# Decays made two units ahead, with two cumulative sums per unit and the third sum replaced by products with w on GpSimd

## The chip, the cores and the metric

The kernel runs on one core of a Trainium2 chip. The metric is the time of one execution on the device in microseconds (us). A profile gives a span, from the first to the last instruction. It is about 1.8 us shorter than the time of the same execution. An execution is called slow when it takes over 1.5% more than the fastest of the same kernel. PE is TensorE (matmuls), DVE is VectorE, ACT is ScalarE, POOL is GpSimd. SBUF is the on-chip memory, PSUM the memory that takes the results of matmuls.

## The reference, cut to what matters

A linear attention with a decay per channel is followed by a two-layer GELU network.

```python
# r, k, v, w: (4 batches, 8 heads, 768 tokens, 48); u: (8, 48); w is between 0.8 and 0.95
for t in range(S):
    cur = einsum('bhd,bhe->bhde', u * k[t], v[t])
    y[t] = einsum('bhd,bhde->bhe', r[t], state + cur)
    state = w[t][..., None] * state + einsum('bhd,bhe->bhde', k[t], v[t])
x = y as (3072 tokens, 384)
out = gelu_tanh(x @ w_in) @ w_out        # w_in 384 x 2048, w_out 2048 x 384
```

## The kernel before

The kernel cuts the work into 12 units, each of 256 tokens of one batch. A partition holds two neighbouring tokens, called t = 0 and t = 1. In a chunk of 128 tokens (64 partitions) the recurrence becomes matmuls: k is divided by the product of the decays up to its token, r is multiplied by it, and the scores are products of the two. The products of decays are exponentials of cumulative sums of log w, and a matmul with a triangular matrix makes such a sum.

For two tokens per partition there are three sums: x (before the first token), y (with the first token), z (with both). The excerpts below show this stage. Cuts are marked with `...`.

```python
def a1(q):                       # PE: three cumulative sums, two matmuls each
    x, y, z = (ps_a.tile([P, 512], FP, ...) for i in range(3))
    for dst, s0, s1 in ((x, strict, strict), (y, incl, strict), (z, incl, incl)):
        PE.matmul(dst[:, 0:HD], s0, lw[:, 0, :, 0:D], start=True, stop=False)
        PE.matmul(dst[:, 0:HD], s1, lw[:, 1, :, 0:D], start=False, stop=True)
    ...
def exps(q):                     # ACT: exp(-y), exp(-z), exp(x), exp(y), and a small one
    ...
def prep(q):
    # DVE: two multiplies of 128x768
    DVE.tensor_tensor(out=kk[:, :, :, 0:D], in0=tdh(kt), in1=dec(e1), op=AL.mult)
    DVE.tensor_tensor(out=rq[:, :, :, 0:D], in0=tdh(rt), in1=dec(fq), op=AL.mult)
    # POOL: v to bf16, k*r, times u, and the decay of the state (am)
    POOL.tensor_copy(out=vb, in_=tdh(vt))
    POOL.tensor_tensor(out=rk, in0=kt..., in1=rt..., op=AL.mult)      # one buffer
    POOL.tensor_tensor(out=rk, in0=rk, in1=u_bc..., op=AL.mult)
    for c2 in range(2):
        POOL.tensor_tensor(out=am[:, c2], in0=blk..., in1=al..., op=AL.mult)
def prep_b(q):                   # DVE: sum over the channels; POOL: times v
    DVE.tensor_reduce(out=dg, in_=rk, axis=AX.X, op=AL.add)
    POOL.tensor_tensor(out=vsc, in0=vb, in1=dg..., op=AL.mult)
def a2(q, which):                # PE: transposes of kk or rq; DVE: copy TT out of PSUM
    ...

for q in range(NU):              # unit q: the network (mm1, mm2); unit q+1: attention
    att = attention(q + 1)       # a2, a2, then scores, y, state, xs, xT
    table("gelu")
    for i in range(8):
        mm1(q, i)                # expansion, 6 matmuls, then a GELU on ACT
        if i >= 2: mm2(q, 0, ...)        # second projection, first half
        next(att) ...
        if i == 6: a1(q + 2)
    table("exp")
    exps(q + 2); ln(q + 3)
    mm2(q, 0, range(12, 16))
    store(q, 0)
    prep(q + 2); prep_b(q + 2)
    mm2(q, 1, range(16))         # 16 matmuls
    store(q, 1)
```

For units 0 and 1 the loop has another order (all eight expansions first), and the weights of the network are cast to bf16 in between.

## Time and profile before

The median is 235.81 us over four runs (235.05 to 238.04).

The first three lines are from the page of the kernel before: busy time of each engine with its share of the span, and two rows of the picture in 40 slices of 5.9 us (tenths of busy PE, tenths of the clock that PE was granted). The clock row reads 9 in the first five slices too, but there the sums' matmuls start 0.32 us apart (23.88 and 24.20 us) where a steady unit has 0.16 us, so PE ran at half speed there and the row does not show it.

```profile
PE 203.4 (86%) x2448; PEld 143.0 (61%) x2448; DVE 131.3 (56%) x211; ACT 134.0 (57%) x223; POOL 104.5 (44%) x87
PE   0456787598895999999999999999999999999992
PEclk9999996779997999999999999999999999999998
```

PE is the busiest engine. Its row shows two parts: about 13 slices in which it often stands still, and a steady part at 9. An average over both hides that the limits differ.

I therefore read from the PE timeline where each unit's first expansion group starts. The differences are the time that each unit takes (its "stretch" below; in the steady part, its "period"):

| kernel before | unit 0 | unit 1 | unit 2 | unit 3 | each of units 3 to 6 | end of span |
|---|---|---|---|---|---|---|
| start, us | 24.8 | 53.7 | 74.0 | 91.3 | 16.56 per unit | 235.9 |

The start takes 91.3 us for three units, and the rest takes 144.6 us for nine. The next line is the windows view of the kernel before for one steady unit: window, its length, busy time of PE, PEld (weight loads), DVE, ACT, POOL with the number of instructions, then the granted clock, the DMA share and GB/s.

```profile
107.90:124.50 16.60, 15.93 (x211) 11.45 (x209) 10.22 (x17) 10.55 (x20) 8.22 (x6) 1.00 0.54 121
```

PE works 15.93 of 16.60 us. The two places where it does not are in the PE timeline of the kernel before (start, duration, instruction, and in brackets the idle time before it and what ended it):

```profile
110.63 0.82 PE L345 MATMUL h_2_1683<-xT_1595,w_in_sb 128*128 128x256 bf16 x6 [0.36 <-ACT g_1644 L347]
118.80 0.32 PE L170 MATMUL cum_1_1847<-logw_122,incl 128*128 128x384 bf16 x1 [0.31 <-ACT xs_1844 L321]
```

The third expansion waits for a GELU, and the second cumulative sum waits for a buffer that the copy of y frees.

These are the two decay multiplies of unit 0 in the kernel before (DVE timeline):

```profile
8.27 0.96 DVE L202 TENSOR_TENSOR kk_125<-k_91,e_219 128x768 bf16<-128x768 f32 x1 [1.04 <-ACT e_219 L184]
9.14 1.58 DVE L203 TENSOR_TENSOR rq_127<-r_93,fq_218 128x768 bf16<-128x768 f32 x1
```

The two are alike in shape and type, yet the second takes 1.58 us and the first 0.96.

### The profile page before, as it was taken

How to read it: one execution, taken by the hardware profiler on the slowest of the kernel's cores; microseconds unless marked ns; L12 is line 12 of the kernel's file. 1: busy time of each engine (PE TensorE's matmuls, PEld its weight loads, DVE VectorE, ACT ScalarE, POOL GpSimd, SP SyncE). 2: the span in 40 equal slices, each digit the busy share in tenths (PEclk: the TensorE clock that was granted, in tenths of full speed). 3: DMA queues.
4: the chain of work that ended last, by engine and by line, in shares of the span. 5: the costliest groups of instructions: out<-in, count | busy, mean ns of one | idle time of the engine just before them, and what ended most of it. 6: DMA issues, size and time to landing. Idle time of an engine off the chain costs nothing.

```text
span 235.9 us, 5759 instructions
## 1 busy us (share of the span) xinstructions
PE 203.4 (86%) x2448; PEld 143.0 (61%) x2448; DVE 131.3 (56%) x211; ACT 134.0 (57%) x223; POOL 104.5 (44%) x87
## 2 busy tenths in 40 slices
PE   0456787598895999999999999999999999999992
PEld 0334564357564767667767667676777677677761
DVE  7684686561636538547547747656285376374200
ACT  3433780566255449459368377395494684765670
POOL 3473792639008504806708509329158076060000
PEclk9999996779997999999999999999999999999998
DMA  7999999713902911942923914915719120020202
GB/s 173 307 396 297 331 320 255 160 33 72 231 15 54 246 25 36 206 98 53 232 56 75 257 24 111 210 33 124 182 35 212 24 62 10 13 56 0 68 1 67
DMA packets 56969, 30.45 MB, mean 129 GB/s; under 512 B 50928, under 2 KB 56176, under 8 KB 56944
## 3 DMA queue, kind: packets, MB, share of 16 engines
q1 hardware_dynamic: 56944, 30.09, 52.1%
q8 instruction: 19, 0.31, 0.6%
q14 instruction: 6, 0.05, 0.1%
HBM read 25.36 MB, written 4.72 MB: 127 GB/s over the span
## 4 chain that ended last, share of the span: by engine, by line
PE 54%; ACT 19%; DVE 11%; issue 9%; POOL 3%; DMA 2%; DVEq 0%; ACTq 0%; POOLq 0%
ACT L156 5%; DVE w_out_sb L86 2%; DMA w_89<-in_w_dram 2%; PE o_0_532 L354 1%; DVE rq_127 L203 1%; ACT logw_124 L162 1%; PE o_0_3678 L354 1%; PE o_0_3457 L354 1%; PE o_0_3175 L354 1%; PE o_1_3740 L354 1%; PE o_1_3632 L354 1%; PE o_1_3389 L354 1%; POOL rk_418 L210 1%; POOL rk_418 L212 1%; ACT logw_122 L162 1%
## 5 line engine op out<-in xcount | busy, mean ns | idle before, releaser
L345 PEld LDWEIGHTS <-w_in_sb 128*128 128x128 bf16 x576 | 54.0, 99 | 21.1 <-issue 9.9
L156 ACT ACT_TABLE_LOAD x13 | 16.7, 1283 | 0.9 <-PEq L487 0.7
L158 ACT ACT_TABLE_LOAD x12 | 15.4, 1283 | 0.2
L171 PEld LDWEIGHTS <-strict 128*128 128x128 bf16 x24 | 2.5, 104 | 9.9 <-issue 9.5
L215 POOL TENSOR_TENSOR am_997<-blk,al_975 128x384 f32<-128x384 bf16 x2 | 2.4, 1230 | 12.5 <-ACT al_975 L187 12.5
L215 POOL TENSOR_TENSOR am_1304<-blk,al_1273 128x384 f32<-128x384 bf16 x2 | 2.4, 1229 | 11.5 <-ACT al_1273 L187 11.5
L215 POOL TENSOR_TENSOR am_1608<-blk,al_1577 128x384 f32<-128x384 bf16 x2 | 2.4, 1230 | 8.3 <-ACT al_1577 L187 8.3
L215 POOL TENSOR_TENSOR am_1912<-blk,al_1881 128x384 f32<-128x384 bf16 x2 | 2.4, 1230 | 8.3 <-ACT al_1881 L187 8.3
L215 POOL TENSOR_TENSOR am_2216<-blk,al_2185 128x384 f32<-128x384 bf16 x2 | 2.4, 1230 | 8.3 <-ACT al_2185 L187 8.3
L215 POOL TENSOR_TENSOR am_2520<-blk,al_2489 128x384 f32<-128x384 bf16 x2 | 2.4, 1228 | 8.3 <-ACT al_2489 L187 8.3
L215 POOL TENSOR_TENSOR am_2811<-blk,al_2780 128x384 f32<-128x384 bf16 x2 | 2.4, 1228 | 7.9 <-ACT al_2780 L187 7.9
L215 POOL TENSOR_TENSOR am_3100<-blk,al_3069 128x384 f32<-128x384 bf16 x2 | 2.4, 1228 | 7.9 <-ACT al_3069 L187 7.9
L215 POOL TENSOR_TENSOR am_3382<-blk,al_3352 128x384 f32<-128x384 bf16 x2 | 2.4, 1228 | 7.9 <-ACT al_3352 L187 7.9
L354 PE MATMUL o_0_532<-w_out_sb,g_437 128*128 128x384 bf16 x16 | 5.5, 469 | 0.2 <-ACT w_out_sb L84 0.2
L236 PEld LDWEIGHTS <-rq_127 128*128 128x128 bf16 x48 | 3.4, 104 | 3.3 <-DVE rq_127 L203 3.2
L354 PEld LDWEIGHTS <-g_437 128*128 128x128 bf16 x32 | 3.3, 117 | 3.2 <-issue 2.5
L170 PE MATMUL cum_0_201<-logw_122,strict 128*128 128x384 bf16 x1 | 0.5, 479 | 5.4 <-ACT logw_122 L162 5.4
L362 DVE COPY ob_3736<-o_0_3678 128x384 f32<-128x384 f32 x1 | 0.6, 558 | 7.7 <-PE o_0_3678 L354 7.7
L215 POOL TENSOR_TENSOR am_699<-blk,al_677 128x384 f32<-128x384 bf16 x2 | 2.3, 1187 | 4.3 <-ACT al_677 L187 4.3
L354 PEld LDWEIGHTS <-g_3653 128*128 128x128 bf16 x32 | 3.0, 98 | 1.7 <-ACT g_3653 L347 0.4
L238 DVE COPY TT_1_818<-T_1_809 128x1024 bf16<-128x1024 bf16 x1 | 0.7, 692 | 6.0 <-PE T_1_809 L236 6.0
L354 PE MATMUL o_0_3678<-w_out_sb,g_3653 128*128 128x384 bf16 x16 | 3.8, 327 | 0.0
(942 smaller groups left out, 694.2 us busy)
## 6 DMA issues: line engine op xcount, KB each, us to landing
wi_155<-in_moe_w_in_dram SPq DMA_DIRECT2D x1, 512.0 KB, 5.0
wi_157<-in_moe_w_in_dram SPq DMA_DIRECT2D x1, 512.0 KB, 6.0
wi_159<-in_moe_w_in_dram SPq DMA_DIRECT2D x1, 512.0 KB, 6.7
wi_161<-in_moe_w_in_dram SPq DMA_DIRECT2D x1, 512.0 KB, 7.5
wi_163<-in_moe_w_in_dram SPq DMA_DIRECT2D x1, 512.0 KB, 8.7
wi_165<-in_moe_w_in_dram SPq DMA_DIRECT2D x1, 512.0 KB, 9.6
w_89<-in_w_dram SPq DMA_DIRECT2D x1, 384.0 KB, 3.7
k_91<-in_k_dram SPq DMA_DIRECT2D x1, 384.0 KB, 4.7
```

Of the source, the lines that this page charges most:

```text
L86: eng.tensor_copy(out=out, in_=in_)
L156: ACT.preload_act_table_set(EXP_SET)
L158: ACT.preload_act_table(AF.Gelu_apprx_tanh)
L162: ACT.activation(out=lw[:, :, :, 0:D].rearrange("p t h d -> p h t d"), in_=ld.pop(("w", q)).rearrange("p h (t d) -> p h t d", t=2), func=A ...
L171: PE.matmul(dst[:, 0:HD], s1, lw[:, 1, :, 0:D], start=False, stop=True)
L203: DVE.tensor_tensor(out=rq[:, :, :, 0:D], in0=tdh(rt), in1=dec(fq), op=AL.mult)
L210: POOL.tensor_tensor(out=rk, in0=kt.rearrange("p h (t d) -> p h t d", t=2), in1=rt.rearrange("p h (t d) -> p h t d", t=2), op=AL.mult)
L212: POOL.tensor_tensor(out=rk, in0=rk, in1=u_bc[:, :, None, :].broadcast_to([P, H, 2, D]), op=AL.mult)
L215: POOL.tensor_tensor(out=am[:, c2], in0=blk.rearrange("p g j d -> p g (j d)"), in1=al[:, :, c2][:, :, None].broadcast_to([P, G, 2 * D]), o ...
L236: PE.transpose(ps[:, g, :, t2, :], src[:, t2, ds(2 * g, 2), :], ident)
L345: PE.matmul(h[:, f, :], w_in_sb[:, cb, ts(ft, P)], xT[:, cb, :], start=(f + cb == 0), stop=(cb == NCB - 1), skip_group_check=True)
L354: PE.matmul(st["o", q, c2], g[:, ft, ts(c2, P)], w_out_sb[:, ft, :], start=(ft == 0), stop=(ft == NFT - 1))
```

## The change

The intent is to relieve PE and ACT in the steady part. exp(-y) is exp(-z) times w of the second token, and exp(y) is exp(x) times w of the first. So the sum y with its two matmuls and two exponentials can go. POOL instead makes k(t=0)·w(t=1) and r(t=1)·w(t=0), called kw and rw, early in the loop. The decays of unit q+3 (before: q+2) are made in loop q, so they are ready a whole unit earlier. The transposes come after the first expansion group, and PE makes all of them, as it did before (the branch for transposes by DMA is never taken). The order of the start changes too. The core of the diff:

```diff
 def a1(q):
-    x, y, z = (ps_a.tile(...) for i in range(3))
+    x, z = (ps_a.tile(...) for i in range(2))
...
+def prep_a(q):
+    POOL.tensor_tensor(out=kw, in0=kt[:, :, 0:D], in1=wt[:, :, D:2 * D], op=AL.mult)
+    POOL.tensor_tensor(out=rw, in0=rt[:, :, D:2 * D], in1=wt[:, :, 0:D], op=AL.mult)
+    POOL.tensor_copy(out=vb, in_=tdh(vt))             # vb now has three buffers
+    ... k*r and times u on POOL, as before (rk, one buffer)
...
 def prep(q):
-    DVE.tensor_tensor(out=kk[:, :, :, 0:D], in0=tdh(kt), in1=dec(e1), op=AL.mult)
-    DVE.tensor_tensor(out=rq[:, :, :, 0:D], in0=tdh(rt), in1=dec(fq), op=AL.mult)
+    for dst, t2, x, dec in ((kk, 0, kw, e1), (kk, 1, kt[:, :, D:2 * D], e1),
+                            (rq, 0, rt[:, :, 0:D], fq), (rq, 1, rw, fq)):
+        DVE.tensor_tensor(out=dst[:, :, t2, :, 0:D], in0=gjd(x), in1=dec..., op=AL.mult)
+    ... am on POOL, as before
...
 table("exp"); ln(0); a1(0)
+prep_a(0)
 exps(0)
 prep(0)
...
 for q in range(NU):
     n = q + 3
-        if i >= 2: mm2(q, 0, (2 * i - 4, 2 * i - 3))
+        if i >= 4: mm2(q, 0, (2 * i - 8, 2 * i - 7))
-        if i == 6 and 0 < q: a1(q + 2)
+        if q > 1: (i == 0: prep_a(n))  (i == 6: a1(n); prep_b(n))
     table("exp")
+    if q == 0: ln(2); ln(3); a1(2); prep_a(2); exps(2)
+    if q == 1: prep_a(3); prep(3); ln(4); a1(4); prep_a(4)
+    if q > 0: exps(n)
+    if q == 0: a1(3); exps(3)
...
     store(q, 0)
+    if q == 0: prep(2); prep_b(2)
+    elif q == 1: prep_b(3); prep(4); prep_b(4)
+    else: prep(n)
     mm2(q, 1, range(16))
```

## The prediction

> **What bounds it now.** The page shows PE busy 86% and every other engine below 58%. The chain of waits gives a steady period of 16.56 us per unit (16.24 later; 14.35 for unit 10, which has no decay stage). In such a period the windows view shows PE busy 15.89, ACT 10.5, DVE 10.2, POOL 8.2 us: the tensor engine is the limit, and ACT touches it at one spot. PE stands still 0.36 us before the third expansion matmul group, because between the last GELU of one unit and the first of the next ACT needs 5.5 us (two table loads of 1.28 us, five exponentials, one Ln), and 0.31 us inside the cumulative sums, for a PSUM buffer that the copy of y frees (timeline). The other limit is the start: unit 3 begins its expansion only at 91.3 us.
>
> **What the change does, costed.**
> - Two 128x384 matmuls less per unit, 0.163 us apart: -0.33 us PE.
> - Two exponentials less: -0.76 us ACT; with 24 instead of 20 second-projection matmuls behind the last GELU, the 0.36 us wait goes.
> - The instruction order shows the second cumulative sum now waiting for the first copy of y, one step older: the 0.31 us goes too.
> - The score matmuls now follow the transposes after a single expansion group. From the start of the transposes to the first score matmul the trace has 1.99 us when nothing else is in between; PE has 0.90 + 0.65 us of work. New wait: about +0.44 us per unit.
> - POOL gets two 128x384 products, an estimated 0.95 us each (half of the 1.81 us for 128x768): not binding. DVE does the same work in four pieces.
> Sum: about -0.6 to -0.75 us per unit for six steady units (about -4). Unit 9 no longer holds a decay stage: -1.5. Unit 10 gets the new wait: +0.4.
>
> **Start.** The first exponentials come 0.65 us earlier, and the output weights are cast after unit 1's masks, not before its transposes: the expansion of unit 1 should begin about 3 us earlier than 53.7. Part is given back. In unit 1's loop the decays of unit 4 wait for a table load and an Ln just before (about 2 us of idle PE). And unit 4's k-r-u product has one buffer: it waits for unit 3's reduction, which waits for an output copy; DVE then stands at unit 4's reduction in front of the transposed copies of unit 3. Two products of 1.81 us: PE should stall about 3 us in unit 2, and the Trainium skill ("TensorE: Matmul & The Clock Gate", Part 1) says that the clock halves after an idle window of about 3.4 us; this trace agrees (after 2.4 us of idle at 74 us an expansion group takes 1.1 us, not 0.66). Net at the start of unit 3's expansion: about -1 us.
>
> **Prediction:** 230.0 us, 8 in 10 between 225.5 and 234.5. Faster by over 2%: 0.58; within 2%: 0.40; slower: 0.02.
>
> **Signs.** Steady period 15.8 to 16.0; no PE wait for GELU in the third expansion group nor inside the cumulative sums; a PE wait of 0.4 us on the second transposed copy in each unit; in unit 2 a wait of about 3 us on that copy, led back to POOL's k-r product; unit 3's expansion starting at 90 us.
>
> **What would make it wrong.** A half clock lasting through units 1 and 2 (slower by up to 4 us); no stall in unit 2 (faster by 3 to 4); steady savings below 0.3 us because the removed waits reappear as waits on DVE.

## The result, and the profile after

The changed kernel is correct and takes 245.85 us (median of four runs, 245.27 to 246.9). Its ratio to the kernel before is 1.042 (95% interval 1.035 to 1.049), so it is slower. A ratio here is the mean time of one kernel's fast runs over that of the other's of the same rounds, so it is not quite the ratio of the medians quoted.

The page of the changed kernel, with the same three lines as above:

```profile
PE 198.8 (82%) x2424; PEld 142.6 (59%) x2424; DVE 151.8 (62%) x236; ACT 125.2 (51%) x199; POOL 127.9 (52%) x111
PE   1254593689887929989989899898998998999993
PEclk9999999758977967999999999999999999999999
```

PE and ACT have less work, as intended. DVE has gained 20.5 us of busy time, though it has the same multiplies as before, in four pieces instead of two. The pieces account for about 3.6 us of it (an estimate: 12 units, four times 0.55 us in place of twice 0.95). The rest is mostly the same multiplies taking longer: their durations sum to 45.6 us in this trace and to 26.1 in that of the kernel before. The idle slices and the low clock are in the first 16 slices. The unit starts say where the time went:

| | unit 0 | unit 1 | unit 2 | unit 3 | steady period | unit 3 to the end |
|---|---|---|---|---|---|---|
| before | 24.8 | 53.7 | 74.0 | 91.3 | 16.56 | 144.6 |
| after | 29.7 | 59.2 | 82.5 | 104.4 | 15.77 | 139.4 |
| difference | +4.9 | +5.4 | +8.4 | +13.0 | -0.79 | -5.2 |

(The differences are taken before rounding.) The steady part gained 5.2 us, about as predicted. The start lost 13.0 us. The difference of the two profiled spans is +7.8 us. The medians differ by 10.0, because the profiled run of the kernel before was one of its longer ones (237.72 us).

The steady part of the changed kernel, in the windows view and the PE timeline:

```profile
104.00:120.00 16.00, 15.34 (x210) 11.34 (x208) 11.73 (x19) 10.09 (x17) 10.62 (x10) 1.00 0.56 126
```

```profile
107.39 0.24 PE L266 MATMUL mt_0_0_1444<-TT_1_1416,TT_0_1405 48*64 48x128 bf16 x2 [0.66 <-ACT g_1396 L368]
114.39 0.49 PE L172 MATMUL cum_1_1609<-logw_122,incl 128*128 128x384 bf16 x2
```

Both old waits are gone: the second cumulative sum has no bracket, and no expansion waits for a GELU. In their place the first score matmul waits 0.66 us. The profile names a GELU as the releaser, but the score matmul reads TT_1, whose copy on DVE ends at 107.34 us (106.66 plus 0.68), and the matmul starts at 107.39.

Now the start. The decay multiplies of unit 0 in the changed kernel, with the GpSimd work of the same time (DVE and POOL timelines):

```profile
9.05 1.22 DVE L231 TENSOR_TENSOR kk_125<-kw_211,e_221 128x384 bf16<-128x384 f32 x1
10.20 2.15 DVE L231 TENSOR_TENSOR kk_125<-k_91,e_221 128x384 bf16<-128x384 f32 x1
12.28 2.16 DVE L231 TENSOR_TENSOR rq_128<-r_93,fq_220 128x384 bf16<-128x384 f32 x1
14.36 1.18 DVE L231 TENSOR_TENSOR rq_128<-rw_212,fq_220 128x384 bf16<-128x384 f32 x1
...
9.04 0.82 POOL L190 CAST vb_215<-v_95 128x768 bf16<-128x768 f32 x1 [0.50 <-DMA v_95<-in_v_dram]
9.83 2.12 POOL L192 TENSOR_TENSOR rk_217<-k_91,r_93 128x768 f32<-128x768 f32 x1
12.02 2.01 POOL L194 TENSOR_TENSOR rk_217<-rk_217,u_bc 128x768 f32<-128x768 f32 x1
13.99 2.24 POOL L236 TENSOR_TENSOR am_230<-blk,al_222 128x384 f32<-128x384 bf16 x2
```

Four multiplies of half the size end at 15.54 us, where two of full size ended at 10.72. Those 4.8 us are nearly all of the +4.9 us of unit 0. Elsewhere in the same trace (unit 2's multiplies, from 57.23 us) each takes 0.55 us and the next starts 0.47 us after it did. None of the slow ones shows idle time before it: the delay is inside its own duration. Each of them overlaps POOL instructions: the first three POOL instructions end at 9.86, 11.95 and 14.03 us, and the first three multiplies at 10.27, 12.35 and 14.44, 0.40 to 0.41 us later.

The same pattern returns in unit 2, where it costs most. These are POOL, DVE and PE lines from the timelines of the changed kernel:

```profile
81.16 2.05 POOL L192 TENSOR_TENSOR rk_1031<-k_436,r_438 128x768 f32<-128x768 f32 x1 [8.89 <-DVE dg_1053 L202]
83.29 2.00 POOL L194 TENSOR_TENSOR rk_1031<-rk_1031,u_bc 128x768 f32<-128x768 f32 x1
85.25 1.79 POOL L203 TENSOR_TENSOR vsc_1054<-vb_998,dg_1053 128x768 bf16<-128x768 bf16 x1
...
80.99 0.55 DVE L231 TENSOR_TENSOR kk_126<-kw_1025,e_1035 128x384 bf16<-128x384 f32 x1
81.45 2.17 DVE L231 TENSOR_TENSOR kk_126<-k_436,e_1035 128x384 bf16<-128x384 f32 x1
83.55 2.16 DVE L231 TENSOR_TENSOR rq_128<-r_438,fq_1034 128x384 bf16<-128x384 f32 x1
85.63 1.83 DVE L231 TENSOR_TENSOR rq_128<-rw_1026,fq_1034 128x384 bf16<-128x384 f32 x1
...
90.04 0.32 PE L266 MATMUL mt_0_0_1145<-TT_1_1117,TT_0_1106 48*64 48x128 bf16 x2 [5.21 <-DVE TT_1_1117 L249]
```

The three POOL instructions end at 83.21, 85.29 and 87.04 us. The three slow multiplies end at 83.62, 85.71 and 87.46, each 0.41 to 0.42 us later. The reading that fits these ends: a multiply does nothing until the POOL instruction is over, then runs, and the next one meets the next POOL instruction. The first multiply, which starts before POOL does, takes 0.55. PE waits 5.21 us for the transposed copy behind all this, and the expansion group after the wait runs at half clock (1.46 us instead of 0.82).

The Trainium skill describes this in "SBUF — State Buffer", section "Who interferes with whom": VectorE and GpSimd share one pair of ports as an exclusive lock, and a VectorE instruction with two SBUF inputs contends with a GpSimd instruction that reads SBUF. It adds: "Issue order, not op shape, decides who blocks." The numbers above agree. The page also says that a reduction on this chip never contends. The trace agrees: the reduction at the end of this stall (87.39 us) took 0.94 us while POOL worked on am, as it does when POOL is idle. Nor were the mask multiplies of this trace stretched, which read one input from PSUM: 0.69 and 0.68 us each between 67.41 and 69.89 us, with POOL busy all that time. But the multiplies are not the only work that is stretched: two casts of weights from SBUF to SBUF took 2.29 and 1.82 us beside POOL work (26.89 and 29.57 us), against 0.68 us in run e1.

### The profile page after: what moved, and what is told of

It reads as the page before. It is cut to its first block, busy times and chain, and to the rows that moved or that the text cites. A ratio compares the mean times of both kernels' runs of the same rounds, so it can differ in the third digit from the quotient of the medians.

```text
span 243.7 us, 5726 instructions
## 1 busy us (share of the span) xinstructions
PE 198.8 (82%) x2424; PEld 142.6 (59%) x2424; DVE 151.8 (62%) x236; ACT 125.2 (51%) x199; POOL 127.9 (52%) x111
## 4 chain that ended last, share of the span: by engine, by line
PE 60%; DVE 5%; ACT 2%; issue 0%; DVEq 0%; ACTq 0%
DVE rq_128 L231 2%; PE o_1_3754 L375 1%; PE o_0_1815 L375 1%; PE o_0_3708 L375 1%; PE o_0_3286 L375 1%; PE o_0_3012 L375 1%; PE o_0_1510 L375 1%; PE o_1_3646 L375 1%; PE o_0_3529 L375 1%; PE o_1_3403 L375 1%; PE o_1_3160 L375 1%; PE o_1_2877 L375 1%; PE o_1_2587 L375 1%; PE o_1_2282 L375 1%; PE o_1_1977 L375 1%; PE o_1_1672 L375 1%
## 5 line engine op out<-in xcount | busy, mean ns | idle before, releaser
L159 ACT ACT_TABLE_LOAD x12 | 15.4, 1283 | 0.2
L375 PE MATMUL o_0_579<-w_out_sb,g_445 128*128 128x384 bf16 x16 | 5.0, 456 | 6.1 <-DVE w_out_sb L86 6.1
L375 PEld LDWEIGHTS <-g_445 128*128 128x128 bf16 x32 | 3.4, 112 | 8.8 <-issue 7.5
L172 PEld LDWEIGHTS <-strict 128*128 128x128 bf16 x24 | 2.0, 106 | 8.0 <-issue 6.5
L192 POOL TENSOR_TENSOR rk_1031<-k_436,r_438 128x768 f32<-128x768 f32 x1 | 2.1, 2053 | 8.9 <-DVE dg_1053 L202 8.9
L203 POOL TENSOR_TENSOR vsc_575<-vb_404,dg_574 128x768 bf16<-128x768 bf16 x1 | 1.7, 1727 | 9.4 <-DVE dg_574 L202 9.4
L248 PEld LDWEIGHTS <-kk_125 128*128 128x128 bf16 x32 | 2.4, 107 | 5.4 <-DVE kk_125 L231 5.3
L375 PEld LDWEIGHTS <-g_777 128*128 128x128 bf16 x32 | 3.6, 122 | 3.1 <-issue 2.0
L375 PE MATMUL o_0_906<-w_out_sb,g_777 128*128 128x384 bf16 x16 | 5.4, 487 | 0.0
L248 PE MATMUL T_0_235<-ident,kk_125 128*128 128x128 bf16 x8 | 1.2, 305 | 5.0 <-DVE kk_125 L231 5.0
L338 ACT ACTIVATE xs_367<-y_0_302 128x384 bf16<-128x384 f32 x1 | 0.5, 492 | 9.0 <-PE y_1_303 L294 9.0
L266 PE MATMUL mt_0_0_1145<-TT_1_1117,TT_0_1106 48*64 48x128 bf16 x8 | 0.6, 310 | 5.2 <-DVE TT_1_1117 L249 5.2
L248 PEld LDWEIGHTS <-rq_128 128*128 128x128 bf16 x48 | 3.2, 104 | 2.4 <-DVE rq_128 L231 2.4
L266 PEld LDWEIGHTS <-TT_0_1106 48*64 48x64 bf16 x32 | 0.8, 154 | 5.9 <-DVE TT_1_1117 L249 5.5
L203 POOL TENSOR_TENSOR vsc_299<-vb_215,dg_298 128x768 bf16<-128x768 bf16 x1 | 1.5, 1482 | 5.2 <-DVE dg_298 L202 5.2
L172 PEld LDWEIGHTS <-incl 128*128 128x128 bf16 x24 | 2.8, 115 | 2.4 <-issue 1.4
L375 PEld LDWEIGHTS <-g_3667 128*128 128x128 bf16 x32 | 3.1, 98 | 1.6
L338 ACT ACTIVATE xs_647<-y_0_582 128x384 bf16<-128x384 f32 x1 | 0.5, 492 | 7.0 <-PE y_0_582 L294 7.0
```

Source lines behind the costliest of these rows:

```text
L159: ACT.preload_act_table(AF.Gelu_apprx_tanh)
L172: PE.matmul(dst[:, 0:HD], tri, lw[:, t2, :, 0:D], start=(t2 == 0), stop=(t2 == 1))
L192: POOL.tensor_tensor(out=rk, in0=kt.rearrange("p h (t d) -> p h t d", t=2), in1=rt.rearrange("p h (t d) -> p h t d", t=2), op=AL.mult)
L203: POOL.tensor_tensor(out=vsc, in0=vb, in1=dg.rearrange("p h t -> p t h")[:, :, :, None].broadcast_to([P, 2, H, D]), op=AL.mult)
L248: PE.transpose(ps[:, :, g, t2, :], src[:, g, t2, :, :], ident)
L266: PE.matmul(mts[j][ds(64 * c2, 64), gi, t2, :], kT[ds(64 * j, D), c2, g, t2, :], rT[ds(64 * j, D), c2, g, :, :], start=(gi + t2 == 0), sto ...
```

## The experiments

There were twelve runs, all with a correct result. Their names begin with e1 to e12. The theory, "exclusion" below: the decay multiplies on DVE and the GpSimd work cannot run at the same time, and the change makes them meet in the start. Rivals: the number of pieces costs it; the products by w fill POOL; the two engines share bandwidth, so that only the amount of work counts; the order of the start is wrong in itself (where unit 4's work and its logarithm stand).

| run | median us | ratio to before (95%) | unit 0 | unit 3 | steady period |
|---|---|---|---|---|---|
| before (first batch) | 235.81 | 1 | 24.8 | 91.3 | 16.56 |
| after | 245.85 | 1.042 (1.035 to 1.049) | 29.7 | 104.4 | 15.77 |
| e1_gate_unit0 | 240.08 | 1.014 (1.008 to 1.020) | 23.8 | 98.8 | 15.77 |
| e2_unit4_out | 243.40 | 1.032 (1.023 to 1.041) | 29.8 | 94.9 | 15.77 |
| e3_split_before | 237.54 | 1.002 (0.995 to 1.009) | 24.2 | 90.6 | 16.56 |
| e4_three_sums | 241.35 | 1.022 (1.016 to 1.027) | 23.4 | 100.9 | 15.72 |
| e5_best | 220.47 | 0.930 (0.923 to 0.938) | 23.7 | 86.5 | 15.05 |
| e6_best_nogate | 250.9, three of four runs slow | none | 30.6 | 97.4 | 17.12 |
| e7_best_late | 222.99, one of four runs slow | 0.941 (0.937 to 0.946) | 23.6 | 84.4 | 15.39 |
| e8_ln4 | 243.23 | 1.027 (1.022 to 1.033) | 29.8 | 103.4 | 15.77 |
| e9_fix_three | 241.64, three of four runs slow | none | 23.6 | 99.3 | 15.77 |
| e10_best_three | 218.65 | 0.925 (0.921 to 0.930) | 23.1 | 81.8 | 15.37 |
| e11_nogate_again | 246.96 | 1.044 (1.038 to 1.050) | 30.9 | 98.8 | 17.12 |
| e12_mixed | 217.62 | 0.919 (0.914 to 0.923) | 23.1 | 81.6 | 15.05 |

The columns "unit 0" and "unit 3" are starts of the expansion in each run's profile. The runs come from several batches on different chips; each ratio is to the kernel before in the same batch, whose median was between 235.8 and 237.5 us. So a difference of medians across batches carries up to 1.7 us of that.

### e1: unit 0's GpSimd work behind the multiplies

Here no wait is removed; one is added. A one-element memset (a "gate" below) by DVE into the buffer that POOL fills next puts POOL's work after the multiplies.

```diff
-prep_a(0)      # kw, rw, vb, k*r, times u
+prep_a1(0)     # kw, rw only
 exps(0)
 prep(0)        # the four multiplies, then, inside it:
+    DVE.memset(vb[:, 0, 0, 0:1], 0.0)
+    POOL.tensor_copy(out=vb, ...); ... k*r; times u; am
```

> The changed kernel, but GpSimd's copy of v, k*r*u products and am of unit 0 are held back (a one-element memset by VectorE on the tile they write) until VectorE has issued the four decay multiplications of unit 0. Theory (GpSimd's instruction and VectorE's two-SBUF-input multiply exclude each other, instruction by instruction): in the changed kernel the four multiplications take 9.05 to 15.54 us; here each takes 0.55 us and the last ends near 11.5; unit 0's expansion starts near 25.5 instead of 29.7, and the whole takes about 4 us less, 241.5. Rival (the start is late because the multiplications wait for the new products k*w and r*w, or because four short strided instructions are slow in themselves): the multiplications still end after 14 us and the time stays at 245 to 246 or gets worse, since GpSimd starts its other work later.

The DVE timeline of this run:

```profile
9.12 0.56 DVE L243 TENSOR_TENSOR kk<-kw,e 128x384 bf16<-128x384 f32 x1
9.60 0.55 DVE L243 TENSOR_TENSOR kk<-k,e 128x384 bf16<-128x384 f32 x1
10.07 0.55 DVE L243 TENSOR_TENSOR rq<-r,fq 128x384 bf16<-128x384 f32 x1
10.54 0.55 DVE L243 TENSOR_TENSOR rq<-rw,fq 128x384 bf16<-128x384 f32 x1
```

The multiplies start where they did and are through at 11.09 instead of 15.54 us. Unit 0's expansion starts at 23.8 instead of 29.7, and the total falls by 5.8 us, both a little more than expected. The theory held, and this one overlap is more than half of the loss. Unit 1's multiplies still met GpSimd in this run (0.57, 1.17, 2.16, 2.16 us), and so did unit 4's (0.55, 2.17, 2.16, 1.83 us).

### e2: unit 4's multiplies and reduction moved into unit 2's loop

```diff
 # q == 1:
-    prep_b(3); prep(4); prep_b(4)
+    prep_b(3)
 # q == 2, at i == 3:
+    prep(4); prep_b(4)
 # q == 2: prep_a(5) at i == 4 (was i == 0), prep_b(5) after prep(5)
```

> The changed kernel, but the decay multiplications and the reduction of unit 4 are taken out of the end of unit 1 and stand in unit 2's loop, behind unit 3's masks. Theory (VectorE's queue is the cause of the 5.2 us stall of PE in unit 2: it stands at multiplications that GpSimd blocks and at a reduction that waits for GpSimd, and unit 3's transposed copies stand behind): the wait for the second transposed copy in unit 2 falls from 5.2 us to about 1, the stretch from unit 2's to unit 3's expansion from 21.9 us to 16 or 17, the time by 4 to 6 us, to about 240.5. Rival (the stall is a data chain of its own, or the half clock): the stretch stays above 20 us.

Unit 2's stretch fell from 21.9 to 15.4 us as hoped. But the stretch of unit 3 rose from 15.8 to 22.2, because there the multiplies of unit 5 (1.75, 2.17, 1.18, 1.18 us) met GpSimd's k·r·u and am. PE then waited 4.4 us for the transposed copy. The total gained 2.5 us by the medians, less than the 4 to 6 expected. In this kernel, moving a blocked piece of work elsewhere helped only where GpSimd was idle in the new place.

### e3: the kernel before, with each multiply cut in two

```diff
-DVE.tensor_tensor(out=kk[:, :, :, 0:D], in0=tdh(kt), in1=dec(e1), op=AL.mult)
-DVE.tensor_tensor(out=rq[:, :, :, 0:D], in0=tdh(rt), in1=dec(fq), op=AL.mult)
+for dst, x, d in ((kk, kt, e1), (rq, rt, fq)):
+    for t2 in range(2):
+        DVE.tensor_tensor(out=dst[:, t2, :, 0:D], in0=tdh(x)[:, t2], in1=dec(d)[:, t2], op=AL.mult)
```

> The kernel before, with each of its two decay multiplications cut in two (four of 128x384 as in the changed kernel, same layout and operands otherwise). Theory of exclusion per instruction: each boundary lets a GpSimd instruction in, so in unit 0, where GpSimd runs the copy of v and two products, the multiplications take some 2 us more (1.0 plus 1.6 become about 4.5 in sum), and in the steady units, where they overlap with GpSimd's am, they grow from 0.95 to 1.1 to 1.2 per half for one or two of the four; the time goes up by 1 to 4 us. Rival (GpSimd and VectorE share bandwidth, so only the amount of work counts): no change beyond 0.5 us.

The time did not change, so my expectation missed, and the number is the one that the rival (shared bandwidth) had forecast. The halves start earlier (7.33 us instead of 8.27, because the first needs only the first exponential) and are through at 10.29 us, just after GpSimd's k·r starts (9.84). Only one of them was blocked, by the cast of v. The trace tells the two theories apart where the time does not. In a steady unit the halves took 0.56, 0.55, 0.55 and 1.19 us. The third had begun (123.50 us) when GpSimd's am started (123.82 us) and was not stretched by it; the fourth, which came second, was. Shared bandwidth should have stretched both. DVE's extra 0.6 us per unit did not count, because DVE is not the limit there. So the number of pieces did not cost time by itself; what counts is which pieces meet GpSimd work.

### e4: the changed kernel with three sums, five exponentials and no products by w

```diff
-x, z = ...; kw, rw on POOL; e1 = exp(-z), fq = exp(x)
+x, y, z = ...; no kw, rw;   e1 = exp(-y), exp(-z), fq = exp(x), exp(y)
```

> The changed kernel's schedule, with the arithmetic of before put back: three cumulative sums, five exponentials, no products k*w and r*w on GpSimd. If the steady gain (16.56 to 15.77 us per unit) comes from the removed matmuls (0.33) and from the reordering (the rest): the steady period is about 16.1 us. If the arithmetic gave it all, it goes back to 16.5. For the start: the theory of exclusion expects unit 0 to stay late (four multiplications against GpSimd's copy and products): unit 0's expansion at 28 to 30 us, against 24.8 before; the rival that blames the products with w expects it back at 25.

Two things came out, and both numbers missed. In the start the theory had unit 0 at 28 to 30 us and the rival that blames the products by w had it at 25. It began at 23.4 us, on the rival's side. The multiplies of unit 0 ran at 7.8 to 10.4 us, before GpSimd's k·r (9.95) could block more than one of them, so they had little to meet. The products by w do harm there, and the trace of the changed kernel shows how: while they run on GpSimd, they block two small DVE copies (0.65 and 0.96 us instead of 0.17), the multiplies start 1.25 us later, and so run into the rest of the GpSimd work. Without the products unit 3 still began at 100.9 us, so they account for about 3.5 of the 13.0 us there.

In the steady part the period is 15.72 us, below both values (16.1 and 16.5) and no longer than the 15.77 with two sums. The two matmuls less (0.33 us) were given back: with three sums PE waits only 0.28 us for the transposed copy, with two sums 0.66. The whole steady gain of the change came from its order of work, none from its arithmetic.

### e5, e6 and e11: a rebuilt order with every overlap gated, and the same without the gates

This kernel keeps the two sums, the products and the decays of unit q+3. It puts the k·r·u work, the cast of v and am behind the multiplies in all units, makes the transposes from unit 3 on inside the second half of the second projection, casts the output weights on ACT and POOL instead of DVE, and makes the decays and multiplies of units 2 and 3 at the end of unit 0. The core:

```diff
+def prep_p(q):                           # after the multiplies of unit q
+    DVE.memset(rk[:, 0, 0, 0:1], 0.0)    # the gate; e6 and e11 leave this line out
+    POOL: k*r, times u, vb, am
...
     store(q, 0)
+    prep_m(n); prep_p(n)                 # multiplies, then the gated GpSimd work
-    mm2(q, 1, range(16))
+    mm2(q, 1, range(8))
+    a2(q + 2, 0); a2(q + 2, 1)           # transposes here, not after the first expansion
+    mm2(q, 1, range(8, 16))
```

> The changed kernel with its start and its GpSimd order rebuilt: in every unit GpSimd's k*r*u products, copy of v and am come after VectorE's four multiplications of that unit (held by a one-element memset), the reduction of unit n moves one loop later, unit 3's multiplications move from the end of unit 1 to the end of unit 0, unit 4's Ln too, all output-weight casts go to ACT and GpSimd before unit 1's attention, second-projection matmuls fill the first two loops, and from unit 3 on the transposes stand inside the second half of the second projection, so that nothing waits for their copies. Theory of exclusion: no multiplication over 0.6 us in the steady units and in units 2 to 4; unit 0's expansion at 23.8 as with the first gate; no PE stall over 1 us in unit 2 or 3; steady period 15.1 to 15.3 us (15.77 less the 0.66 us wait for the transposed copy). Time 221 to 226 us. If the stalls have another cause, a wait of several us remains in units 1 to 3 and the time stays above 232.

> The same kernel without the one-element memsets, so that GpSimd may run its products while VectorE multiplies; the order on each engine is otherwise equal. Theory of exclusion: the multiplications of unit 0 stretch again (to about 5 to 6 us in sum, because GpSimd's products start as soon as r is there), unit 0's expansion comes 3 to 5 us later; in the steady units GpSimd's products start some 4 us before the multiplications are through and each multiplication waits for one of them (1.2 to 2.2 us instead of 0.55), about 4 to 5 us more on VectorE's queue per unit, behind which the transposed copies stand: steady period 0.3 to 2 us longer. Rival (the gate itself is worth nothing): within 1 us of the gated kernel.

> The rebuilt kernel without the one-element memsets, once more: three of its four runs were called slow, so no ratio was given. Theory: with overlap allowed the four multiplies take 5 us in sum instead of 2.2, the steady period is 16.5 to 17.2, and the fast runs are at 246-247 us (ratio about 1.04). If the long times were the slow state alone, fast runs would be at 222-230 us with a period near 15.1-15.6.

With the gates the kernel takes 220.47 us, 7% less than the kernel before and just under the range expected. Two points of that expectation missed: unit 4's first multiply took 1.33 us, and PE stood 1.82 us in unit 2 for the transposed copy. Without the gates the first try gave no ratio; its profile, a slow run, had unit 0 at 30.6 us, 6.9 us later than with gates, where 3 to 5 were expected. The repeat (e11, the same kernel to the letter) took 246.96 us, all fast, and met its expectation. The four multiplies of a steady unit, in the DVE timeline, first with gates (e5), then without (e11):

```profile
128.91 0.56 DVE L245 TENSOR_TENSOR kk<-kw,e 128x384 bf16<-128x384 f32 x1
129.38 0.55 DVE L245 TENSOR_TENSOR kk<-k,e 128x384 bf16<-128x384 f32 x1
129.85 0.55 DVE L245 TENSOR_TENSOR rq<-r,fq 128x384 bf16<-128x384 f32 x1
130.32 0.55 DVE L245 TENSOR_TENSOR rq<-rw,fq 128x384 bf16<-128x384 f32 x1
```

```profile
130.82 0.69 DVE L244 TENSOR_TENSOR kk<-kw,e 128x384 bf16<-128x384 f32 x1
131.44 2.16 DVE L244 TENSOR_TENSOR kk<-k,e 128x384 bf16<-128x384 f32 x1
133.52 1.17 DVE L244 TENSOR_TENSOR rq<-r,fq 128x384 bf16<-128x384 f32 x1
134.61 1.18 DVE L244 TENSOR_TENSOR rq<-rw,fq 128x384 bf16<-128x384 f32 x1
```

With the gates the four take 1.96 us from start to end, without them 4.97. The list of PE's waits of e11 (total us, times, longest) shows what PE pays:

```profile
PE mt L274 <- DVE TT L257: 20.9, 10, 5.7
```

The period is 15.05 against 17.12 us, and unit 0 starts at 23.7 against 30.9. A memset of 0.06 us per unit, the only line in which the two kernels differ, separates 220.47 from 246.96 us. The two ran in different batches; their ratios to the kernel before are 0.930 and 1.044. This is the clearest test of the theory. The slow runs of e6 are not used for it.

### e7: the rebuilt kernel with the transposes at the changed kernel's place

```diff
-A2 = 3      # from unit 3 on, transposes inside the second projection of loop q - 2
+A2 = NU     # transposes after the first expansion group of loop q - 1
```

> The rebuilt kernel with gates, but the transposes at the changed kernel's place, behind the first expansion group, directly in front of the score matmuls. If the wait for the transposed copy is the cost of that place: the steady period is 0.4 to 0.5 us longer than in the rebuilt kernel (1.99 us from transposes to scores against 0.90 + 0.65 us of other work), 15.6, and the time 3 to 4 us longer. With the multiplications out of the way the wait is 0.44 us as predicted, not the 0.66 us of the changed kernel.

The period rose by 0.34 to 15.39 us, less than the 0.4 to 0.5 expected (15.6 had been named). PE's idle time before the scores was 0.28 us, not 0.44. The time rose by 2.5 us where 3 to 4 were expected: the part after unit 3's start grew by 3.7 us, but unit 3 began 2.1 us earlier than in e5. The period's distance to the changed kernel's 15.77 is 0.38 us, just the difference of the two waits for the transposed copy (0.66 and 0.28). It fits that am no longer meets the rq multiplies, which took 1.19 and 1.18 us there and take 0.55 here; the runs do not separate the gates from the other changes of order. In e5 the transposes' new place then fills the wait that is left.

### e8: the logarithm of unit 4 taken at the end of unit 0

```diff
 if q == 1: prep_a(3); prep(3)
-    ln(4)
 ...
 if q == 0: a1(3); exps(3)
+    ln(4)
```

> The changed kernel with one edit: the logarithm of unit 4's decays is taken at the end of unit 0 instead of in the middle of unit 1's last stretch. Theory: the 1.8 us in which the tensor engine waits there for this logarithm, and the half clock after it (eight matmuls at 0.32 us each instead of about 0.16), are a loss of their own: unit 1's period falls from 23.3 to 20-21 us, total 2 to 3.5 us faster than the changed kernel (ratio to the kernel before 1.028 to 1.034). Rival: VectorE is the limit through units 1 and 2, so an earlier logarithm only lengthens the stall of unit 2, and the total stays within 1 us (ratio 1.04).

Unit 1's stretch fell from 23.3 to 19.6 us, somewhat more than expected, and the 24 second-projection matmuls behind the sums ran at full clock (4.06 us for the group). But unit 1 began 2.1 us later in this profile (1.7 us of it were there before the moved instruction), and unit 2's stretch grew by 0.7. The span fell by only 1.0 us (243.7 to 242.7), the median by 2.6. The ratio to the kernel before, 1.027 (1.022 to 1.033), lies on the side of the theory (1.028 to 1.034) and not of the rival (1.04), and the profiled run was the slowest of four. So the loss was real, but its size in the total stays open between 1 and 3.5 us.

### e9: three repairs of the changed kernel together

The gates of e1 in units 0, 3 and 4, unit 4's reduction in unit 2's loop, and the early logarithm of e8.

```diff
+GATED = (0, 3, 4)   # vb, k*r, times u behind the multiplies in these units
-    prep_b(4)        # at the end of q == 1
+    prep_b(4)        # q == 2, i == 3
-    ln(4)            # q == 1
+    ln(4)            # end of q == 0
```

> The changed kernel with three repairs and nothing else: in units 0, 3 and 4 GpSimd's k*r*u work waits for the decay multiplies (a one-element memset by VectorE), unit 4's reduction moves into unit 2's loop, and unit 4's logarithm is taken at the end of unit 0. Theory (overlap of VectorE multiplies with GpSimd instructions in the start is what failed in the prediction): the three losses are repaired together: unit 0's expansion at about 24, unit 3's at 90-95 us, steady period still 15.77, total 231-236 us, ratio 0.975 to 1.0. Rival (the order of work of the change is itself too long for VectorE and GpSimd, overlap or not, so the stall moves on as it did when unit 4's work was moved alone): unit 3's expansion not before 97 us, total 238 or more.

This fell on the side of the rival. Unit 0 was repaired (23.6), but unit 3 began only at 99.3 us. One fast run took 238.01 us; the three others (241.62 to 241.76) are called slow, so there is no ratio. The only profile is of a slow run, so the 99.3 us and the lines below show where this kernel stalls, but not how long it stalls in a fast run. Three lines of its DVE and PE timelines:

```profile
75.66 0.95 DVE L215 TENSOR_REDUCE dg<-rk 128x16 f32<-128x768 f32 x1 [3.74 <-POOL rk L207]
78.19 1.33 DVE L244 TENSOR_TENSOR kk<-kw,e 128x384 bf16<-128x384 f32 x1 [1.57 <-POOL kw L193]
83.94 0.64 PE L284 MATMUL mt<-TT,TT 48*64 48x128 bf16 x16 [7.81 <-DVE TT L267]
```

Exclusion was gone for unit 3's multiplies (0.55 us each), though not for unit 1's and the first two of unit 4's. And the gated order put GpSimd's whole product between two pieces of DVE work: DVE stood 3.74 us for it, then 1.57 us for kw, and the transposed copies came after all of that. PE stood 7.81 us. So a gate is no cure by itself. The pieces behind it (the reduction here) must also be moved to where nobody waits for them, as e5 does.

### e10 and e12: three sums in the rebuilt kernel, throughout or in the start only

```diff
+three = q <= LAST3          # e12: LAST3 = 4; e10: three sums in all units
-x, z: two sums; kw, rw on POOL
+x, y, z: three sums, five exponentials, no kw, rw (where three is true)
```

> The rebuilt kernel with three cumulative sums and five exponentials, without the products by w. In the changed kernel the two saved matmuls (0.33 us) were given back by a longer wait for the transposed copy. In the rebuilt kernel that wait is filled. Theory: here the saved matmuls count: steady period 15.35-15.4 instead of 15.05, total 2 to 4 us longer than the rebuilt kernel run beside the same kernel before (ratio about 0.945). Rival: another engine sets 15.05, and the period stays within 0.1 of it (ratio 0.93).

The period was 15.37 as the theory said: where PE is the limit, two matmuls count fully (0.32 us). But the total did not rise as expected. At 218.65 us it was no slower than e5's 220.47 (the intervals of the two ratios overlap), because unit 3 began at 81.8 instead of 86.5 us. In e5, kw of unit 4 had been queued on GpSimd behind other work, and that unit's first multiply waited 1.73 us for it and then took 1.33 us against rw. That led to the mixed version:

> The rebuilt kernel with three sums for units 0 to 4 and two sums with the products by w from unit 5 on. The rebuilt kernel began unit 3's expansion at 86.5 us and had a period of 15.05; with three sums throughout it began at 81.8 and had 15.37. Theory (the products by w delay VectorE and GpSimd in the start, where these are the limit, and save tensor-engine time in the steady part, where that engine is the limit): unit 3 at 81.5-83 us, periods 15.05 from unit 5 on, span about 215 us (81.8 plus the 133.1 us that the rebuilt kernel took from there, an estimate), total 216-218 us, ratio to the kernel before 0.912 to 0.922. Rival (the 4.7 us at the start was the order of the instructions in that run or the clock of that chip): unit 3 at 84-87 us, total 219-221 us.

It came out as expected: unit 3 at 81.6, period 15.05, span 214.6, time 217.62 us, 8% less than the kernel before. Its ratio's interval still touches that of e10, so its lead over three sums throughout rests on the period in the profiles (unit 3 begins 0.3 us earlier, which single profiles cannot tell from noise). The page line and a steady window of e12:

```profile
PE 190.1 (89%) x2434; PEld 138.5 (65%) x2434; DVE 130.9 (61%) x245; ACT 131.3 (61%) x212; POOL 107.3 (50%) x101
```

```profile
111.70:126.70 15.00, 15.00 (x207) 11.16 (x206) 10.93 (x20) 9.79 (x16) 9.32 (x9) 1.00 0.57 133
```

PE is now busy all of a steady unit. The clock that it was granted averages 1.000 in this profile, against 0.968 in that of the kernel before: from about 24 us on PE never falls back to half clock. Before that this average counts as full what the trace shows at half: the sums of unit 1 still start 0.32 us apart there (21.61 and 21.93 us).

## Why the prediction was wrong

**What bounds the kernel: right.** PE was the limit in the steady part, with the two waits named.

**The steady part: right in sum, partly by luck.** The period came out at 15.77 us; 15.8 to 16.0 was predicted. Both old waits went. The new wait on the transposed copy came, at 0.66 us instead of 0.44: in the trace the rq multiplies met am, took 1.19 and 1.18 us, and the copies came later. The term "-0.33 us PE" was real work saved but no time saved, as e4 showed (15.72 with three sums). It was worth its 0.33 only once the wait behind it was filled (e5 against e10). That the sum came out all the same is luck: the new order was worth more than its terms. Unit 9 gained 1.3 us (1.5 predicted), and unit 10 lost 0.2 (0.4 predicted). From unit 3 to the end the gain was 5.2 us, against about 5 predicted.

**The step that failed: the start, "Net at the start of unit 3's expansion: about -1 us".** It was +13.0 us: 4.9 before unit 0's expansion, 0.5 in unit 0's stretch, 3.0 in unit 1's and 4.6 in unit 2's. The false terms in it are two sentences of the costing: that POOL's products are "not binding" and that "DVE does the same work in four pieces". Both took each engine's work by its duration when alone. Run beside each other, a 0.55 us multiply took up to 2.17 us. A third false term has nothing to do with exclusion: that the later casts of the output weights would help (first point). This is where it shows:

- Unit 0 was predicted to make unit 1 start about 3 us earlier. Its multiplies took 6.5 us in place of 2.5, and unit 0 itself began 4.9 us later. With the overlap taken away (e1) it began 5.9 us earlier than in the changed kernel. The other ground for those 3 us failed too: with the output weights cast later, PE stood 3.67 and then 2.38 us for DVE's casts (the two lines below this list, PE timeline of the changed kernel), where the kernel before stood 2.07 us for the transposed copy behind them and 2.73 us for a logarithm. In the first of these waits DVE worked through the masks and a reduction, with GpSimd idle until shortly before its end, so exclusion is not its cause.
- The unit-2 stall was predicted, with its place, its cause in the one buffer and the half clock after it, but at 3 us. It was 5.21 us. The prediction counted GpSimd's two products. It did not count that DVE's multiplies could not run meanwhile and had to end one by one behind them.
- Unit 1's stretch, where about 2 us of idle PE was predicted, was longer by 3.0 us: a wait of 1.81 us for the logarithm, and a half clock around it.

```profile
43.05 0.80 PE L375 MATMUL o_0_579<-w_out_sb,g_445 128*128 128x384 bf16 x2 [3.67 <-DVE w_out_sb L86]
49.36 0.60 PE L375 MATMUL o_0_579<-w_out_sb,g_445 128*128 128x384 bf16 x2 [2.38 <-DVE w_out_sb L86]
```

How much of the 13.0 us is exclusion is not shown. Gating unit 0 returned 5.6 us at unit 3's start. What remains against the kernel before (98.8 against 91.3) is shared by the exclusion that e1 left in place (units 1 and 4), the order of DVE's and GpSimd's work in units 1 and 2, the logarithm, and the output-weight casts. I could not split this further: single repairs were given back in the next unit (e2, e8), and the joint repair made a new stall (e9, profiled in a slow run). That the start as a whole can be made short with the same arithmetic is shown by e5, which reached unit 3 at 86.5 us; but e5 also reordered the matmuls and the casts of units 0 and 1, and without its gates (e11) unit 3 began at 98.8 us.

The range was wrong for the same reason: "slower" had a chance of 0.02, because the list of risks held only the clock and the steady waits. The trace of the kernel before had the warning: rq in 1.58 us beside kk in 0.96, the same shape.

## What to carry to other kernels

When two like instructions of VectorE show different durations in one trace, look at what GpSimd runs at that time before you cost any work moved between the two. Cost such moves as if the two engines were one wherever a two-input SBUF multiply meets GpSimd work, as the 0.55 us multiplies here that took up to 2.17, and order them with a cheap dependency (a one-element memset) so that the short urgent piece runs first, then move whatever waits for the long piece off the path too. An arithmetic saving counts only on the engine that sets the period in that stage: here the same two matmuls were worth 0.33 us per unit or nothing, and it paid to use a different formula in the start than in the steady part.

## What the Trainium skill lacked or had wrong

- "SBUF — State Buffer", "Who interferes with whom", has the rule and the runs agree with it, but it does not say how blocking looks in a profile: as idle time or inside the instruction. Here the blocked time is inside the VectorE instruction's own duration (0.55 us becomes 1.17 to 2.17), with no idle time before it. The GpSimd instruction is lengthened too (1.81 becomes 2.00 to 2.12 us for 128x768; a pair of am products 1.62 becomes 2.24).
- The same page does not say that back-to-back instructions on both engines take turns: in unit 2 of the changed kernel, three multiplies each ended 0.41 to 0.42 us after one GpSimd instruction. Nor does it show how an order can be forced. Here a memset of 0.06 us per unit separated 220.47 from 246.96 us.
- "Perfetto Trace Analysis", "Optimizing Scalar/DVE Operations", says that offloading between GpSimd and VectorE might not help, and gives no size. The gates move no work between the two, but they show what overlap can cost: the rebuilt kernel without gates took 12% longer than with them (246.96 over 220.47, medians of two batches).
- "TensorE: Matmul & The Clock Gate", Part 1, ties the half clock to an idle window of about 3.4 us. In the kernel before, the clock fell at 74 us after 2.37 us of idle PE, and an expansion group then took 1.10 us from start to start, not 0.66. In the changed kernel the clock fell at 70 us when the longest single wait in the ten microseconds before was 0.93 us, and PE was busy for 1.92 of the last 4 us. The page tells of re-throttling through short idles too, but gives no busy share at which it starts. The windows view of the changed kernel (columns as above; the clock is the third number from the end):

```profile
66.00:68.00 2.00, 1.07 (x35) 0.69 (x34) 1.50 (x3) 0.00 (x0) 1.92 (x3) 1.00 1.28 262
68.00:70.00 2.00, 0.85 (x25) 0.51 (x26) 1.89 (x4) 0.00 (x0) 2.00 (x4) 1.00 0.72 147
70.00:72.00 2.00, 2.00 (x34) 1.33 (x35) 0.30 (x1) 0.49 (x1) 2.00 (x3) 0.52 0.03 8
```
